# Low parts by accumulating DMAs, another place for M, and a table for side work, in a gated mix of linear attention and FNet

## The chip, the cores and the metric

The kernel runs on one core of one Trainium2 chip. The time is the device time of one execution in microseconds (us), the median of the runs shown. PE is TensorE, DVE is VectorE, ACT is ScalarE, POOL is GpSimd, SP is SyncE, which here only issues DMAs. A row such as `L748 PE MATMUL bank<-pk,c` is an instruction of line 748 of the kernel before; names are those of its tiles.

## The reference

S = 2048 tokens, D = 576, 32 heads of 18. All in float32.

```python
g = sigmoid((x * gate_w).sum(-1))
qkv = (x @ wqkv) split into q, k, v of 32 heads
phi = lambda t: where(t > 0, t + 1, exp(t)) + 1e-6
pq, pk = phi(q), phi(k)
kv = einsum("bhsd,bhse->bhde", pk, v); z = pk summed over s
o = einsum(pq, kv) / (einsum(pq, z) + 1e-6)
a = o @ wo
y = dft_seq_re @ (x @ dft_hid_re.T) - dft_seq_im @ (x @ dft_hid_im.T)
return g * a + (1 - g) * y
```

## The kernel before, in words

A float32 number is kept as two fp32r parts: `hi` (ACT copies the number into a tile of that type) and `lo` (DVE subtracts `hi` from the number). A product of two such numbers is three passes on PE: hi hi, hi lo, lo hi. Large products are built from seven smaller ones on sums of quarters: `Left` makes the seven left operands from pieces `xb` of x, `right_here` and `Hidden.make_w` the right operands `wb` and `wf`. The stages, in the order of time:

- **k'** (to about 65 us): x (tiles `xs`) times the key weights `wd`, sixteen tiles of 128 tokens, with phi on ACT and DVE, into `acc` (k' as numbers, for z) and `pk` (its parts).
- **k'^T x** (65 to 132 us): `pk` against x in the other layout, `c`, in 20 steps: five columns c by four quarters q. x comes by SP as `craw` and is split into `c`. Beside the steps runs side work: the sum of k' over its tiles (`zacc`, then `z_chain` and `z_sum`), the right operands of q (the three generators `wq_pieces`, a, b, c), the left operand `here[NP]` (p: its last rows go by SP from `xb` to a DRAM scratch, `xr<-xb`, and are read back as `rests[p]`, `xr<-xr`), the left operand of p = 6 (x), and the loads of Wo. `turn` says which generator is pushed at which step, `plan` what else is done there. `kv_step` multiplies by the value weights.
- **q** (129 to 195 us): 56 slots, eight pieces p by seven products (`q_product`, L913), each on two `xb` or `xf` parts and on `rests[p]`. Between slots stand, by a second `plan`, the making of kv, of M = kv Wo (`build_m` into `mf`), the moves of M's rows from `mf` into a layout of 128 rows by DMA (`move_m`; SP and POOL), M's parts (`split_m`), the left operands 7, 0 and 1 (`begin_left`, `left`), the loads of `rests` (`load_rest_q`), and the steps of the division by the denominators (`norm`, `pz`, `den`).
- **M** (195 to 263 us): sixteen tiles, transposed `acc` (`qs`, split into parts) times M (`mw`), evicted by ACT with the gate and stored to `att` by POOL. Beside them `Hidden.make_w` splits the seven right operands `wf` of the hidden transform, one at a tile; those of 3 to 6 lie over `acc` tiles that have been stored.
- **Hidden and sequence transforms** (263 us to the end).

The order of rows on each engine is that of the code after a scheduler that keeps dependencies; POOL and SP each issue their DMAs in order. `lo_later` puts a subtraction on a list that `tick` empties. The generators yield between pieces, `go` pushes one by a step. Of places: a tile is bound to an address (`at`), so two tiles at one address wait for each other. In q, M's raw rows lie at T_AT + 25856 and 35072, over the sums `sets` of the first slots; `mf` lies at T_AT, where `begin_left(1)` puts the pieces of left operand 1; `rests[6]` and `rests[2]` of the step table lie over the temporaries of piece c.

Of the kernel before, what the change touches and what calls it, by code (L numbers as in the profile page):

```python
# [8 lines left out]
F = mybir.dt.float32  # L9
R = mybir.dt.float32r  # L10
# [126 lines left out]
def kernel(  # L137
# [112 lines left out]
    acc = [at(ACC_AT + i * D * 4, [P, D], F, "acc") for i in range(NT)]  # L250
# [305 lines left out]
    pace()  # L556
# [52 lines left out]
    zacc = at(CONST_AT + 3584, [P, D], F, "zacc")  # L609
    for i in range(FT, NT):  # L610
# [12 lines left out]
        if i in (10, 12, 14):  # L623
            add(zacc, zacc if i > 10 else acc[0], acc[i // 2 - 4])
# [86 lines left out]
    def load_forms(p, o, queue=nc.sync):  # L711
        t = forms[p] = at(o, [P, 7, 2, 2 * P], R, "xf")
        for a, b in ((2, 4), (0, 2), (4, 6), (6, 7)):
            queue.dma_start(out=t.bitcast(F)[:, a:b], in_=xforms[p][:, a:b])
# [8 lines left out]
    turns = dict(p=rest_forms(), a=wq_pieces[0], b=wq_pieces[1], c=wq_pieces[2], x=left_of(6, False))  # L723
    turn = {4: "p", 5: "p", 6: "p", 7: "p", 8: "pap", 9: "pa", 10: "pax", 11: "pxa", 12: "paxc",
            13: "pcbx", 14: "xbc", 15: "bc", 16: "b", 17: "b"}

    plan = {
        2: [lambda: begin_left(NP, ACC_AT)],
        6: [z_chain, lambda: begin_left(6, ACC_AT + 22784)],
        8: [z_sum, lambda: go(wq_pieces[1]), lambda: go(wq_pieces[2])],  # L730
        12: [lambda: load_wo(2)],
        14: [lambda: load_forms(2, ACC_AT + 8448, nc.gpsimd), lambda: load_wo(3)],
        16: [lambda: wo_split[2](lo_later), lambda: load_rest_q(6, SLOT_AT + 40320)],
        17: [lambda: wo_split[3](lo_later), lambda: load_rest_q(2, SLOT_AT + 43904)],
# [4 lines left out]
    for c in range(5):  # L739
        ps = [bank(), bank()]  # L740
        passes = FULL if c < KC else FULL[:2]
        for q in range(NCU):
# [17 lines left out]
            for i in (2 * step + 4, 2 * step + 5):  # L760
                if i < NT:
                    add(zacc, zacc, acc[i])
            for f in plan.get(step, ()):
                f()
            left_part()
            for k in turn.get(step, ""):
                go(turns[k])
# [6 lines left out]
    for f in turns.values():  # L774
        go(f, 9)
# [30 lines left out]
    def scale(t, d):  # L806
# [3 lines left out]
        o = (SLOT_AT + (14336 if t < 3 else 48256) if t < 4 else T_AT + 36864) + t % 8 * 512  # L810
# [55 lines left out]
    def move_m(g, queue=nc.sync):  # L866

        if not ms:
            ms["raw"] = at(T_AT + 25856, [P, KC, D], F, "mraw")
            ms["rest"] = at(T_AT + 35072, [P, D], F, "mraw")  # L870
        mraw, mrest = ms["raw"], ms["rest"]
# [621 lines left out]
```

## Time and profile before

| | before |
|---|---|
| runs, us | 730.86 to 732.08, median 731.05 |
| the profiled execution, us | 731.42 |
| its span, us | 729.6 |
| around the span, us | 1.8 |
| PE busy | 719.6 us, 99% |
| DVE, ACT, POOL busy | 597.3, 329.6, 56.8 us |
| DMA | 211 GB/s over the span |
| mean PE clock | 0.997 of full |

A row of the timeline has start, duration, engine, line, operation and tiles; in brackets stands how long the engine was idle before it, and what it waited for. In a DMA row the last figure is the median time from issue to landing. The numbers of the windows are busy us (x instructions) of PE, PE's weight load, DVE, ACT and POOL, then PE's granted clock, the share of the DMA engines and GB/s.

### The profile page before, as it was taken

The page shows a single profiled execution, that of the slowest core. Times are in us where ns is not written, and L with a number is a line of the kernel's source. Part 1 is how long each engine was busy: PE and PEld are TensorE (multiplying, and loading weights), DVE is VectorE, ACT ScalarE, POOL GpSimd, SP SyncE. Part 2 cuts the span into 40 slices and gives each one's busy share as a digit, 9 for nine tenths or more (in the row PEclk, how much of TensorE's full clock was granted, in tenths as well). Part 3 has the DMA queues.
Part 4 walks back from the last instruction along what each step waited for, and adds up shares of the span by engine and source line. Part 5 has one row for each costly group of instructions (what it writes and reads, how often), then busy time and mean ns, then how long its engine had stood idle before and what let it go on. Part 6 is the DMA issues. An engine that isn't in the chain of part 4 may idle for free.

```text
span 729.6 us, 13716 instructions
## 1 busy us (share of the span) xinstructions
PE 719.6 (99%) x5390; PEld 715.8 (98%) x5390; DVE 597.3 (82%) x996; ACT 329.6 (45%) x506; POOL 56.8 (8%) x101
## 2 busy tenths in 40 slices
PE   9999999998999999999999999999999999999997
PEld 9999999998999999999999999999999999999997
DVE  5799987577999848979999889857888987788884
ACT  6898346575545544443344334323535332232230
POOL 1111221122041100000000000000000000000000
PEclk9999999999999999999999999999999999999999
DMA  7384798984279648454476666889964544544540
GB/s 255 115 279 163 246 302 296 396 276 175 102 260 384 263 147 329 130 161 137 155 247 175 223 240 199 290 308 400 374 198 132 159 140 141 159 150 144 153 152 33
DMA packets 51516, 156.66 MB, mean 215 GB/s; under 512 B 6212, under 2 KB 8676, under 8 KB 50428
## 3 DMA queue, kind: packets, MB, share of 16 engines
q1 hardware_dynamic: 42268, 116.43, 47.3%
q0 software_dynamic: 8896, 38.95, 14.7%
q8 instruction: 43, 0.70, 0.4%
q10 hardware_dynamic: 288, 0.41, 0.2%
q14 instruction: 21, 0.17, 0.1%
HBM read 117.80 MB, written 36.49 MB: 211 GB/s over the span
## 4 chain that ended last, share of the span: by engine, by line
PE 76%; DVE 10%; DMA 9%; issue 2%; ACT 1%; SPq 1%; POOL 1%; DVEq 0%; POOLq 0%; ACTq 0%
PE bank L1270 41%; PE bank L1115 14%; PE bank L209 14%; DMA xr<-xr 2%; DVE c L189 2%; PE bank L913 2%; PE bank L748 2%; PE bank L571 2%; DVE craw L199 1%; DVE fl L189 1%; DMA wraw<-in_wq_rest_dram 1%; DMA craw<-in_xg_dram 1%; DMA xm<-xb 1%; DVE ys L199 1%; PE bank L828 1%
## 5 line engine op out<-in xcount | busy, mean ns | idle before, releaser
L1270 PE MATMUL bank<-fh,c 128*128 128x288 f32 x1792 | 356.1, 295 | 0.4 <-DVE c L189 0.4
L1270 PEld LDWEIGHTS bank<-fh,c 128*128 128x128 f32 x1792 | 286.0, 188 | 1.0 <-DVE c L189 0.9
L1270 PE MATMUL bank<-fl,c 128*128 128x288 f32 x896 | 263.2, 294 | 0.4 <-DVE fl L189 0.4
L179 ACT ACTIVATE c<-craw 128x1792 fp32r<-128x1792 f32 (+1 forms) x84 | 121.6, 1448 | 192.8 <-DVE craw L199 158.4
L1270 PEld LDWEIGHTS bank<-fl,c 128*128 128x128 f32 x896 | 168.7, 188 | 1.1 <-DVE fl L189 0.9
L189 DVE TENSOR_TENSOR c<-craw,c 128x1792 fp32r<-128x1792 f32 (+4 forms) x86 | 141.9, 1653 | 1.7 <-ACT c L179 1.6
L199 DVE TENSOR_TENSOR craw<-craw 128x256 f32<-128x256 f32 (+1 forms) x192 | 98.3, 512 | 24.3 <-DMA craw<-in_ci_dram 13.0
L1115 PE MATMUL bank<-wf,xf 128*128 128x288 f32 x630 | 98.5, 296 | 0.0
L1115 PEld LDWEIGHTS bank<-wf,xf 128*128 128x128 f32 x630 | 90.0, 189 | 0.0
L209 PE MATMUL bank<-mw,qs 128*128 128x288 f32 x448 | 63.5, 298 | 0.8 <-DVE qs L189 0.5
L748 PE MATMUL bank<-pk,c 128*128 128x288 f32 x448 | 62.1, 296 | 0.8 <-ACT c L179 0.4
L748 PEld LDWEIGHTS bank<-pk,c 128*128 128x128 f32 x448 | 60.1, 188 | 1.5 <-DVE c L189 0.8
L209 PEld LDWEIGHTS bank<-mw,qs 128*128 128x128 f32 x448 | 60.0, 188 | 1.4 <-DVE qs L189 0.7
L209 PE MATMUL bank<-wd,xs 128*128 128x288 f32 (+1 forms) x336 | 44.7, 295 | 0.0
L209 PEld LDWEIGHTS bank<-wd,xs 128*128 128x128 f32 x336 | 44.6, 188 | 0.0
L199 DVE TENSOR_TENSOR ys<-bank,ys 128x288 f32<-128x288 f32 x63 | 28.8, 456 | 17.3 <-PE bank L1270 14.3
L189 DVE TENSOR_TENSOR fl<-fl,fh 128x864 fp32r<-128x864 f32 (+1 forms) x32 | 34.6, 1092 | 6.8 <-ACT fh L179 5.2
L179 ACT ACTIVATE fh<-fl 128x864 fp32r<-128x864 f32 (+1 forms) x32 | 29.8, 949 | 16.2 <-DVE fl L199 16.2
L1115 PE MATMUL bank<-wf,xr 96*128 96x288 f32 x112 | 33.3, 298 | 0.0
L199 DVE TENSOR_TENSOR ys<-ys,bank 128x288 f32<-128x288 f32 x47 | 21.1, 450 | 13.5 <-PE bank L1270 12.9
L1292 ACT ACTIVATE ys<-bank 128x288 f32<-128x288 f32 x16 | 6.6, 412 | 53.2 <-PE bank L1270 53.2
L1333 ACT ACTIVATE acc<-bank,gate 128x288 f32<-128x288 f32 x32 | 15.9, 502 | 29.7 <-PE bank L209 29.6
(131 smaller groups left out, 802.1 us busy)
## 6 DMA issues: line engine op xcount, KB each, us to landing
xf<-xm SPq DMA_DIRECT2D x49, 512.0 KB, 9.0
craw<-in_cr_dram SPq DMA_DIRECT2D x32, 512.0 KB, 3.8
craw<-in_ci_dram SPq DMA_DIRECT2D x32, 512.0 KB, 4.2
xr<-xr SPq DMA_DIRECT2D x20, 448.0 KB, 8.2
xm<-xb POOLq DMA_DIRECT2D x8, 1024.0 KB, 5.2
xm<-xb POOLq DMA_DIRECT2D x8, 768.0 KB, 7.1
craw<-in_xg_dram SPq DMA_DIRECT2D x20, 256.0 KB, 5.9
att<-acc POOLq DMA_DIRECT2D x16, 288.0 KB, 3.5
```

What stands on the lines that cost most here:

```text
L179: return nc.scalar.activation(dst, src, AF.Copy, bias=bias)
L189: nc.vector.tensor_tensor(out=dst, in0=src, in1=hi, op=ALU.subtract)
L199: nc.vector.tensor_tensor(out=dst, in0=a, in1=b, op=op)
L209: nc.tensor.matmul(ps, a, b, start=(n == 0), stop=(n == len(pairs) - 1))
L571: nc.tensor.matmul(ps[i], x[:, i * P:(i + 1) * P], wkt.row(h, j), start=(c == 0 and n == 0), stop=(c == KC and n == 1))
L748: nc.tensor.matmul(ps[h][:, :HALF], t[:, a, k], pk[s][:, b, half(h)], start=(s == 0 and n == 0), stop=(s == NT - 1 and n == len(passes) - 1))
L828: nc.tensor.transpose(banks[c // KC][:, (c % KC) * P:(c % KC + 1) * P], a, ident)
L913: nc.tensor.matmul(ps, a, b, start=(start and n == 0), stop=(stop and n == len(ops) - 1), skip_group_check=True)
L1115: nc.tensor.matmul(ps, a, b, start=(start and n == 0), stop=(n == len(ops) - 1), skip_group_check=True)
L1270: nc.tensor.matmul(ps[q], c[x][:, l, k], factors[p](y, f), start=(p == 0 and i == 0), stop=(p == NP - 1 and i == 2))
L1292: nc.scalar.activation(c11, ps[1], AF.Copy)
L1333: done.append(nc.scalar.activation(acc[i][:, half(h)], ps[:, :HALF], AF.Copy, scale=gate[:, t:t + 1]))
```

## The change

- **`lo_by_dma`**: the low part is made without DVE. ACT writes -hi into its place, and POOL issues a DMA that adds the raw number there. In `Hidden.make_w` it replaces DVE's fourteen subtractions of Wr's parts, one of 128 x 576 and one of 32 x 288 for each of seven; the sixth `make_w` goes from tile 12 to 13.
- **M**: raw rows go to T_AT + 14336 and 23552 (Wo's pieces 0, 1 and 4 lay there), all at slot 14 (before: 18 and 19). Its parts are made by chunk pairs: hi at slots 21 and 24, the rest at 28, the low parts by -hi on ACT and an accumulating DMA of 576 KB at 30 and 32 (before: DVE, at 31 and 46).
- **Slots in q**: `begin_left(1)` at 16 (19), `rests` 7 and 1 by SP (POOL), `rests` 5 by POOL ahead of its `xf` forms (SP; the forms were at slot 13, now 15), nine norms instead of ten and earlier ones, two `pz` places instead of four.
- **Sum of k'**: by pairs of tiles (128 x 1152): seven adds and a last one of 128 x 576, instead of fifteen of 128 x 576. `z_chain` stands at step 4 (6), `z_sum` at 7 (8).
- **Side work of k'^T x**: one table `turn` names what is done at each step. The stores of p's rest rows come a step later, piece a ends at step 15 (12). `rests[2]` goes to POOL, ahead of the forms of 2, both at step 16.

**Where the rows stand.** PE, the end of k'^T x and the first q products; `wb` are right operands of q, `xr_203` (after) and `xr_212` (before) are `rests[6]`, `c` the last two chunks of x. Before:

```order
L689 MATMUL bank_987<-gt_211_1636,plain_189_1396 72x72
L748 MATMUL bank_1639<-pk_42_123,c_205_1590 128x288 x2
L748 MATMUL bank_1640<-pk_42_123,c_205_1590 128x288 x2
...
L913 MATMUL bank_1771<-wb_104_481,xb_177_1260 128x288 x3
L748 MATMUL bank_1639<-pk_46_127,c_210_1631 128x288 x2
...
L748 MATMUL bank_1640<-pk_49_130,c_210_1631 128x288 x2
L913 MATMUL bank_1771<-wb_184_1346,xb_177_1260 128x288 x3
L913 MATMUL bank_1771<-wb_186_1350,xr_212_1663 128x288
L913 MATMUL bank_1784<-wb_104_481,xf_206_1592 128x288 x3
```

After:

```order
L703 MATMUL bank_979<-gt_202_1616,plain_177_1370 72x72
L929 MATMUL bank_1758<-wb_180_1374,xb_163_1166 128x288 x2
L929 MATMUL bank_1758<-wb_182_1378,xr_203_1644 128x288
L764 MATMUL bank_1619<-pk_34_115,c_197_1567 128x288 x2
L764 MATMUL bank_1620<-pk_34_115,c_197_1567 128x288 x2
...
L764 MATMUL bank_1619<-pk_41_122,c_201_1607 128x288 x2
L764 MATMUL bank_1620<-pk_41_122,c_201_1607 128x288 x2
L929 MATMUL bank_1771<-wb_96_473,xf_205_1648 128x288 x3
```

The first matmul on `rests[6]` stood behind the last 32 matmuls on `c`; now it stands ahead of them.

SP, the last steps of k'^T x: `xr<-xb` are the stores of the rest rows, `xr<-xr` the loads of `rests` (first the one of 6), `in_xg_dram` x for the steps. Before:

```order
L402 DMA xr_114<-xb_1095 32x4x896
L596 DMA craw_1588<-in_xg_dram 128x512
L662 DMA wraw_1598<-in_wo_dram 128x576
L596 DMA craw_1629<-in_xg_dram 128x512
L709 DMA xr_1663<-xr_114 128x896
L709 DMA xr_1696<-xr_114 128x896
L709 DMA xr_1717<-xr_114 128x896
```

After:

```order
L408 DMA xr_106<-xb_1084 32x4x896 x2
L602 DMA craw_1565<-in_xg_dram 128x512
L408 DMA xr_106<-xb_1084 32x4x896
L676 DMA wraw_1578<-in_wo_dram 128x576
L602 DMA craw_1605<-in_xg_dram 128x512
L723 DMA xr_1644<-xr_106 128x896
L723 DMA xr_1702<-xr_106 128x896
```

The last store stood ahead of the x load that is now ahead of it; the load of `rests[2]` is gone from here to POOL.

SP, in q, where `mf` is the source of M's moves, the last load of forms before them, and the first `xr<-xr` behind is `rests[0]`. Before:

```order
L721 DMA xf_1761<-xm_109 128x1536
L721 DMA xf_1762<-xm_110 128x1536
L709 DMA xr_2045<-xr_114 128x896
L709 DMA xr_2047<-xr_114 128x896
...
L880 DMA mraw_2081<-mf_1741 112x576
L880 DMA mraw_2081<-mf_1741 8x576 x2
L882 DMA mraw_2082<-mf_1741 64x576
```

After:

```order
L735 DMA xf_1749<-xm_102 128x1536
L892 DMA mw_2016<-mf_1726 4x576
L892 DMA mw_2016<-mf_1726 112x576
...
L894 DMA mraw_2017<-mf_1726 64x576
L895 DMA mraw_2017<-mf_1726 64x576
L723 DMA xr_2043<-xr_106 128x896
L723 DMA xr_2244<-xr_106 96x896
L723 DMA xr_2246<-xr_106 128x896
```

Nine moves that stood behind the loads of `rests` 0 and 5 now stand ahead of those of `rests` 0, 7 and 1.

The diff, cut to its core:

```diff
+    def lo_by_dma(dst, src, hi):
+        nc.scalar.activation(dst, hi, AF.Copy, scale=-1.0)
+        nc.gpsimd.dma_start(out=dst.bitcast(F), in_=src, accum_op=ALU.add)
...
-    acc = [at(ACC_AT + i * D * 4, [P, D], F, "acc") for i in range(NT)]
+    pairs = [at(ACC_AT + i * D * 4, [P, 2 * D], F, "acc") for i in range(0, NT, 2)]
+    acc = [pairs[i // 2][:, i % 2 * D:i % 2 * D + D] for i in range(NT)]
...
     zacc = at(CONST_AT + 3584, [P, D], F, "zacc")
+    sums = pairs[4]
+    z_at = {10: 0, 11: 1, 13: 2}
...
             f()
-        if i in (10, 12, 14):
-            add(zacc, zacc if i > 10 else acc[0], acc[i // 2 - 4])
+        if i in z_at:
+            add(sums, sums, pairs[z_at[i]])
...
+    z_left = [3, 5, 6, 7]
+    def z_pair():
+        add(sums, sums, pairs[z_left.pop(0)])
     def z_chain():
+        add(zacc, sums[:, :D], sums[:, D:])
...
-    turns = dict(p=rest_forms(), a=wq_pieces[0], b=wq_pieces[1], c=wq_pieces[2], x=left_of(6, False))
-    turn = {4: "p", 5: "p", 6: "p", 7: "p", 8: "pap", 9: "pa", 10: "pax", 11: "pxa", 12: "paxc",
-            13: "pcbx", 14: "xbc", 15: "bc", 16: "b", 17: "b"}
+    turns = {"p": rest_forms(), "a": wq_pieces[0], "b": wq_pieces[1], "c": wq_pieces[2],
+             "x": left_of(6, False), "L": left_part, "+": z_pair, "S": z_chain, "Z": z_sum,
+             "N": lambda: begin_left(NP, ACC_AT), "X": lambda: begin_left(6, ACC_AT + 22784),
+             "q": lambda: (go(wq_pieces[1]), go(wq_pieces[2]))}
+    turn = ("+L", "L+", "+N", "L", "+LSX", "LpL", "pL", "ZLpL", "pp", "qL", "pax", "axp", "pc", "ppca",
+            "xpacbx", "axbcb", "b", "", "b", "")
...
     plan = {
-        2: [lambda: begin_left(NP, ACC_AT)],
-        6: [z_chain, lambda: begin_left(6, ACC_AT + 22784)],
-        8: [z_sum, lambda: go(wq_pieces[1]), lambda: go(wq_pieces[2])],
         12: [lambda: load_wo(2)],
-        14: [lambda: load_forms(2, ACC_AT + 8448, nc.gpsimd), lambda: load_wo(3)],
-        16: [lambda: wo_split[2](lo_later), lambda: load_rest_q(6, SLOT_AT + 40320)],
-        17: [lambda: wo_split[3](lo_later), lambda: load_rest_q(2, SLOT_AT + 43904)],
+        14: [lambda: load_wo(3)],
+        16: [lambda: wo_split[2](lo_later), lambda: load_rest_q(6, SLOT_AT + 40320),
+             lambda: load_rest_q(2, SLOT_AT + 43904, nc.gpsimd),
+             lambda: load_forms(2, ACC_AT + 8448)],
+        17: [lambda: wo_split[3](lo_later)],
...
                 wvt[c + 1], wv_split = load_pair(wv_ring.next(), wv[:, c + 1])
-            for i in (2 * step + 4, 2 * step + 5):
-                if i < NT:
-                    add(zacc, zacc, acc[i])
+            for k in turn[step]:
+                turns[k]() if k in "+SNXZqL" else go(turns[k])
...
                 f()
-            left_part()
-            for k in turn.get(step, ""):
-                go(turns[k])
...
     tick()
-    for f in turns.values():
-        go(f, 9)
+    for k in "pabcx":
+        go(turns[k], 9)
...
                                        op0=ALU.add, op1=ALU.mult)
-        o = (SLOT_AT + (14336 if t < 3 else 48256) if t < 4 else T_AT + 36864) + t % 8 * 512
+        o = (SLOT_AT + (14336 if t < 3 else 48256) if t < 4 else T_AT + 38912) + t % 4 * 512
...
         if not ms:
-            ms["raw"] = at(T_AT + 25856, [P, KC, D], F, "mraw")
-            ms["rest"] = at(T_AT + 35072, [P, D], F, "mraw")
-        mraw, mrest = ms["raw"], ms["rest"]
+            ms["lo"] = at(T_AT + 14336, [P, KC, D], R, "mw")
+            ms["rest"] = at(T_AT + 23552, [P, D], F, "mraw")
+        mraw, mrest = ms["lo"].bitcast(F), ms["rest"]
...
+    minus = [at(T_AT + o, [P, 2, D], F, "minus") for o in (45568, 60416)]
     def split_m(h, part):
-        if h == 0 and part == 0:
-            ms["hi"] = at(T_AT + 14336, [P, 5, D], R, "mw")
-            ms["lo"] = at(T_AT + 25856, [P, KC, D], R, "mw")
-        mraw, mrest, mhi, mlo = (ms[k] for k in ("raw", "rest", "hi", "lo"))
+        if not part and not h:
+            ms["hi"] = at(T_AT + 25856, [P, 5, D], R, "mw")
+        mraw, mrest, mhi = ms["lo"].bitcast(F), ms["rest"], ms["hi"]
+        cs = slice(2 * h, 2 * h + 2)
         if part == 0:
-            hi_of(mhi[:, :KC, half(h)], mraw[:, :, half(h)])
-            hi_of(mhi[:, KC, half(h)], mrest[:, half(h)])
+            hi_of(mhi[:, cs], mraw[:, cs])
+        elif part == 1:
+            nc.scalar.activation(minus[h], mhi[:, cs], AF.Copy, scale=-1.0)
+            nc.gpsimd.dma_start(out=mraw[:, cs], in_=minus[h], accum_op=ALU.add)
         else:
-            lo_of(mlo[:, :, half(h)], mraw[:, :, half(h)], mhi[:, :KC, half(h)])
-            lo_of(mhi[64:, KC, half(h)], mrest[64:, half(h)], mhi[64:, KC, half(h)])
+            hi_of(mhi[:, KC], mrest)
+            lo_by_dma(mhi[64:, KC], mrest[64:], mhi[64:, KC])
...
     def spread():
-        pz_ring.at = [T_AT + 40960 + k * D * 4 for k in range(4)]
-    m_parts = [lambda: split_m(0, 0), lambda: split_m(0, 1),
-               lambda: split_m(1, 0), lambda: split_m(1, 1)]
+        pz_ring.at = [T_AT + 40960 + k * D * 4 for k in range(2)]
+    m_parts = [lambda a=a: split_m(*a) for a in ((0, 0), (1, 0), (0, 1), (1, 1), (0, 2))]
...
         12: [lambda: build_m((4,))],
-        13: [lambda: load_forms(5, T_AT + 66048, nc.gpsimd)],
-        15: [lambda: load_rest_q(0, SLOT_AT + 40320), lambda: load_rest_q(5, SLOT_AT + 43904)],
-        18: [lambda: move_m(2), lambda: move_m(0, nc.gpsimd), lambda: move_m(3)],
-        19: [lambda: move_m(4), lambda: move_m(1, nc.gpsimd), lambda: begin_left(1, T_AT)],
+        14: [lambda: move_m(2), lambda: move_m(0, nc.gpsimd), lambda: move_m(3), lambda: move_m(4),
+             lambda: move_m(1, nc.gpsimd)],
+        15: [lambda: load_rest_q(0, SLOT_AT + 40320),
+             lambda: load_rest_q(5, SLOT_AT + 43904, nc.gpsimd),
+             lambda: load_forms(5, T_AT + 66048)],
+        16: [lambda: begin_left(1, T_AT)],
...
         30: [spread],
-        31: [lambda: load_rest_q(7, T_AT + 80384, nc.gpsimd),
-             lambda: load_rest_q(1, T_AT + 108928, nc.gpsimd)],
+        31: [lambda: load_rest_q(7, T_AT + 80384), lambda: load_rest_q(1, T_AT + 108928)],
...
     }
-    for k, what in ((7, (10, 11, 13, 15, 17)), (0, (14, 16, 18, 20, 24)), (1, (33, 34, 35, 36, 38)),
-                    (None, (25, 27, 29, 41, 43, 45, 47, 48, 49, 52)), ("m", (30, 31, 45, 46))):
+    for k, what in ((7, (10, 11, 12, 15, 17)), (0, (13, 15, 17, 19, 23)), (1, (30, 33, 34, 36, 38)),
+                    (None, (18, 20, 25, 35, 41, 43, 47, 48, 48)), ("m", (21, 24, 30, 32, 28))):
...
                 f()
-            if k == 51:
+            if k == 52:
...
             hi_of(rl[:96], last)
-            lo_later(w[:, :, 1], raw, w[:, :, 0])
-            lo_later(rl[32:64], last[32:64], rl[32:64])
+            lo_by_dma(w[:, :, 1], raw, w[:, :, 0])
+            lo_by_dma(rl[32:64], last[32:64], rl[32:64])
...
         tick()
-        if i == 0 or 2 < i < 7:
+        if i in (0, 3, 4, 5, 6):
...
                 here[k].store((slice(0, 4), slice(4, 7))[j % 2], done[-1])
-        for k, j in enumerate((7, 8, 9, 10, 11, 12, 14)):
+        for k, j in enumerate((7, 8, 9, 10, 11, 13, 14)):
...
```

More of the change, by code (lines that the diff above doesn't have):

```diff
@@ L555 @@
         load_next()
-    pace()
+    pace(mybir.EngineType.Pool)
     for h in range(2):
@@ L709, in load_rest_q, with load_forms @@
         queue.dma_start(out=rests[p].bitcast(F)[:n], in_=xrest[p * 96:p * 96 + n])
-    def load_forms(p, o, queue=nc.sync):
-        t = forms[p] = at(o, [P, 7, 2, 2 * P], R, "xf")
+    def load_forms(p, o):
+        forms[p] = at(o, [P, 7, 2, 2 * P], R, "xf")
         for a, b in ((2, 4), (0, 2), (4, 6), (6, 7)):
-            queue.dma_start(out=t.bitcast(F)[:, a:b], in_=xforms[p][:, a:b])
+            nc.gpsimd.dma_start(out=forms[p].bitcast(F)[:, a:b], in_=xforms[p][:, a:b])
     def load_two(*places):
```

## The prediction

> **What bounds the kernel now.** I read the page first, then PE's waits by line, then the timeline and the chain at the waits. PE is the bound:
>
> ```profile
> PE 719.6 (99%) x5390; PEld 715.8 (98%) x5390; DVE 597.3 (82%) x996; ACT 329.6 (45%) x506; POOL 56.8 (8%) x101
> ```
>
> No matmul is removed, so only PE's stalls can be won or added. Its waits between 60 and 265 us (us in total, times, longest):
>
> ```profile
> PE bank L913 <- DVE xb L189: 1.1, 1, 1.1
> PE bank L913 <- DMA xr<-xr: 1.1, 2, 0.8
> PE bank L209 <- DVE qs L189: 0.5, 1, 0.5
> PE bank L748 <- ACT c L179: 0.4, 1, 0.4
> PE bank L209 <- ACT qs L179: 0.4, 1, 0.4
> PE bank L748 <- DVE c L189: 0.4, 1, 0.4
> ```
>
> That is 3.9 us, and all that this stretch offers beside a clock loss. The PE timeline (start, duration, idle before) shows the places that matter:
>
> ```profile
> 126.75 2.37 PE L748 MATMUL bank<-pk,c 128*128 128x288 f32 x16
> 131.92 0.30 PE L913 MATMUL bank<-wb,xr 96*128 96x288 f32 x1
> 133.37 0.40 PE L913 MATMUL bank<-wb,xr 96*128 96x288 f32 x1 [0.35 <-DMA xr<-xr]
> 160.07 0.30 PE L913 MATMUL bank<-wb,xr 96*128 96x288 f32 x1
> 174.25 0.96 PE L913 MATMUL bank<-wb,xf 128*128 128x288 f32 x6
> 176.75 0.82 PE L913 MATMUL bank<-wb,xb 128*128 128x288 f32 x4 [1.15 <-DVE xb L189]
> 178.35 0.40 PE L913 MATMUL bank<-wb,xr 96*128 96x288 f32 x1 [0.79 <-DMA xr<-xr]
> 179.91 1.64 PE L913 MATMUL bank<-wb,xf 128*128 128x288 f32 x6
> ```
>
> The same six matmuls take 0.96 us at 174.25 and 1.64 at 179.91: after 1.94 us of waits PE also ran at a lower clock. The windows (PE busy and count first, PEclk third from the end) give its size: 5 x (1 - 0.90) + 5 x (1 - 0.75) = 1.75 us.
>
> ```profile
> 175.00:180.00 5.00, 3.07 (x18) 2.60 (x17) 3.81 (x7) 3.64 (x10) 0.00 (x0) 0.90 0.44 161
> 180.00:185.00 5.00, 5.00 (x31) 5.00 (x31) 4.78 (x11) 3.26 (x8) 0.73 (x2) 0.75 0.01 3
> ```
>
> The waits at 176.75 and 178.35 therefore cost 1.15 + 0.79 + 1.75 = 3.7 us. The chain tells whence they come:
>
> ```profile
> 156.10 0.38 DVE acc L923
> 156.50 0.73 SPq L880
> ...
> 162.19 3.85 DMA mraw<-mf
> 166.81 0.64 POOL xb L366
> ...
> 170.38 7.93 DMA xr<-xr
> 178.35 4.74 PE bank L913 x22
> ```
>
> M's raw rows go onto the place of q sums, which DVE frees at 156.10; the left operand 1 is loaded over their source, so it starts only when they landed.
>
> **The change part by part.** The rows of SP's queue and of landings (KB each, median us to landing) that the terms use:
>
> ```profile
> 114.71 0.52 SPq L402 DMA_DIRECT2D xr<-xb  x1
> 118.22 0.34 SPq L596 DMA_DIRECT2D craw<-in_xg_dram  x1
> 122.77 4.49 SPq L709 DMA_DIRECT2D xr<-xr  x3
> 151.02 1.25 SPq L709 DMA_DIRECT2D xr<-xr  x2
> 156.50 5.07 SPq L880 DMA_DIRECT2D mraw<-mf  x7
> 161.61 0.54 SPq L882 DMA_DIRECT2D mraw<-mf  x1
> 162.19 0.59 SPq L883 DMA_DIRECT2D mraw<-mf  x1
> ...
> xr<-xr SPq DMA_DIRECT2D x20, 448.0 KB, 8.2
> xr<-xb SPq DMA_DIRECT2D x6, 448.0 KB, 7.8
> xr<-xr POOLq DMA_DIRECT2D x1, 336.0 KB, 4.7
> att<-acc POOLq DMA_DIRECT2D x16, 288.0 KB, 3.5
> xf<-xm POOLq DMA_DIRECT2D x6, 512.0 KB, 6.4
> ```
>
> *1. M elsewhere, moved at slot 14: -3.7.* The moves no longer wait for 156.10; they follow slot 14, at about 146 us if the 56 slots fill 129 to 195 evenly, and their region (Wo's pieces, last read at slot 12) is free by then. The xb loads behind them come some 7 us earlier than 166.81, far more than the 1.94 us of waiting, and rests 1 goes out on SP at slot 31, by the same spacing at about 166 us, instead of 170.38. Cover, if it is gone: the old 3.7. Bounds -3.7 and -1.2 (only the wait on xb goes).
>
> *2. SP's nine moves ahead of rests 0: +1.8.* Rests 0 and 5 were issued at 151.02, with the moves behind them; now the nine moves, 5.07 + 0.54 + 0.59 = 6.2 us of SP, come first, and behind them wait the loads of rests 0, 7 and 1 (rests 5 went to POOL). The matmul that reads rests 0 stood at 160.07; 151.02 + 8.2 = 159.2, so 0.9 us were to spare. If the moves start at 147.5 us (an estimate between 146, the even spacing, and 150), rests 0 goes out at 153.7 and lands at 161.9: 1.8 us late. Bounds: 146 gives 0.3; 150 gives 4.3; nothing, if the landing takes the 4.7 us of the 336 KB row.
>
> *3. Rests 6 is read earlier, and its load is later: +3.5, and +1.5 of clock.* In the new order PE meets the first matmul on rests 6 ahead of the last 32 matmuls on c. Their first half stood at 126.75, so PE comes there at 126.75 + 2 x 0.13 = 127.0, not at 131.92. The load waits for the last store xr<-xb. That store stood at 114.71, ahead of the xg load of 118.22; now it stands behind it, at about 118.6. With 7.8 us to landing the load goes out at 126.4 instead of 122.77, and with 8.2 it lands at 134.6: 7.6 us of stall. Other end: the store lands in time, the load goes out at 122.8 and takes 4.7: 127.5, 0.5 us. The xf loads of form 2, ahead of it in POOL's queue before, now leave after it or with it, which speaks for the shorter landings; I take 130.5, a stall of 3.5. The two waits of 1.94 us together were followed by 1.75 us of clock loss, so I add 1.5 (0 to 1.8). The wait of 0.35 at 133.37 goes: rests 2 is on POOL and is read after the 32 matmuls, 4.3 us later: -0.35. Behind PE's wait are queued the 32 matmuls on c, whose operands are ready; they fill no gap, since PE runs in order.
>
> The Trainium skill ("TensorE: Matmul & The Clock Gate", Part 1: The HAM clock gate) puts the drop to half clock at an idle window of some 3.4 us; here it came after two waits of 1.15 and 0.79 us, so the trace is the stricter. By the page the 1.5 us of clock would be nothing for a wait of under 3.4 us, which is rival C below.
>
> *4. z by pairs, and the turn table: -0.2.*
>
> ```profile
> L199 DVE TENSOR_TENSOR zacc<-zacc,acc 128x576 f32<-128x576 f32 x14 | 10.5, 750 | 0.2
> L189 DVE TENSOR_TENSOR mw<-mraw,mw 128x1152 fp32r<-128x1152 f32 x2 | 2.7, 1354 | 0.5 <-ACT mw L179 0.5
> L189 DVE TENSOR_TENSOR wf<-wraw,wf 128x576 fp32r<-128x576 f32 x7 | 5.3, 752 | 3.4 <-ACT wf L179 3.4
> L179 ACT ACTIVATE wf<-wraw 128x576 fp32r<-128x576 f32 x7 | 4.7, 676 | 0.0
> ```
>
> Fifteen adds of 0.75 us become seven of 1.35 (the 128x1152 row) and one of 0.75: 11.2 against 10.2 us, 1 us of DVE less in a stage where PE waited 0.8 us for c. The side work moves some steps later, towards the steps where these waits were. I take a quarter of the 0.8; bounds -0.8 and +0.6 (one more such wait).
>
> *5. M's and the q stage's DVE work: -0.8.* Four DVE lows (2.7 us for two of 128x1152, 0.9 for two of 64x288) go to ACT and POOL, one division step of ten is dropped, and DVE is busy 4.78 of 5 us in 180 to 185. The waits of 0.5 and 0.4 on qs stand at the end of that stretch; I take 0.8 of the 0.9; bounds -0.9 and 0. The replacing ACT copies are three, the two larger twice the 676 ns row's width, and ACT works 3.26 of 5 us there; the accumulating DMAs leave POOL when DMA moves 3 GB/s.
>
> *6. Wr's lows by DMA: +0.3.* Fourteen DVE subtracts (5.3 us for seven, and seven small ones) go; fourteen ACT copies like the 0.68 us row and fourteen POOL issues come, into tiles 7 to 14. There DVE is not late for anything, so their leaving gives nothing:
>
> ```profile
> 230.00:240.00 10.00, 10.00 (x80) 10.00 (x79) 8.64 (x18) 6.73 (x18) 1.62 (x3) 1.00 1.02 416
> ```
>
> DMA, however, is full (share 1.02), and ACT also evicts PE's banks. Four of the new pieces lie over tiles whose store to att must land first; the store stands behind the accumulating DMAs on POOL, and behind the ACT copy that waits stand the evictions. Bounds: 0 where ACT's slack hides it, and 2 x 2.9 = 5.8 where two stores land after 6.4 instead of 3.5 us. I take 0.3, by the 3.3 of 10 us that ACT has free in that window.
>
> The Trainium skill ("Collectives: The Full Stack", Why ReduceScatter is half of AllGather) speaks against this part: an add inside the DMA needs two source reads and so halves the rate. No row of before has an accumulating DMA. By the page 288 KB would go like 576 KB, nearer to the 6.4 us than to the 3.5 us row, and the term would be nearer 3 than 0.3.
>
> The other moves (transposes one group later, first products of the next stage ahead of the last tile, norms at other slots, a pz ring of two) change the order within a PE that is full there: 0, within 0.3 either way.
>
> **Sum.** -3.7 + 1.8 + 3.5 + 1.5 - 0.35 - 0.2 - 0.8 + 0.3 = +2.05 us. The profiled execution took 731.42 us (span 729.6 and 1.8 around it), 0.37 above the median of 731.05; so 733.5 for such an execution, and 733.1 for the median.
>
> **The rivals.** *A: both rests are in time (faster).* If stores and loads land in 5 rather than 8 us, since fewer transfers share the queues, the stall at rests 6 is 0.5 to 1, rests 0 costs nothing and the clock stays: -3.7 + 0.7 - 0.35 - 0.2 - 0.8 + 0.3 = -4.05, 727.0. It decides at a landing of rests 6 before 128.5 us. For it: the 4.7 us row; against: 20 loads of this kind with a median of 8.2. Chance 0.27. *B: the accumulating DMAs take double* and hold ACT in tiles 9 to 14: +2.05 + 4, 737.1. It decides where a store lands over 6 us after its issue. Chance 0.11. *C: the stalls come, but the clock stays*, as it would where a single wait of 3.5 us is too short to lower it: +2.05 - 1.5 = +0.55, 731.6, no change; against it the 0.75 of the window after two shorter waits. Chance 0.14. *D: the change doesn't do what it says*: the moves are still held, by SP or by their region, and the waits at 176.75 and 178.35 stay: +5.7, 736.8. Against it: the new place is free after slot 12. Chance 0.06. My forecast keeps 0.42.
>
> **How the numbers follow.** Likeliest: 733.1 us. A difference of 0.2% (1.46 us) is about what a measurement of this kernel can tell from no change: faster is below 729.6, slower above 732.5. Of the forecast's 0.42, 0.33 lie above, 0.06 within, 0.03 below (term 3 alone runs from 0.5 to 7.6); of C's 0.14, 0.12 within and 0.02 below. Faster 0.27 + 0.03 + 0.02 = 0.32; same 0.06 + 0.12 = 0.18; slower 0.33 + 0.11 + 0.06 = 0.50. Signs are mixed, so the forecast's own range, with the bounds of terms 2 and 3, is 731.5 to 738. The range for all reaches from A's 727.0 less 0.5 to B with term 3 in its middle: 726.5 to 738.5.
>
> **What would show it.** Term 1: no wait near 176 to 178 and PEclk 1.00 in 180 to 185. Term 2: a PE wait on xr near 160 after an SP issue at 153 or later. Term 3: a PE wait on xr near 127 ahead of 32 matmuls on c, and a clock under 1 behind it. Term 5: no wait on qs near 199. Term 6: no PE wait on ACT in 230 to 260, and landings of wf<-wraw near 3.5 us. The prediction is wrong if rests 6 lands before PE comes to it, or if ACT is held in the tiles.

## The result and the profile after

| | before | after |
|---|---|---|
| median of five runs, us | 730.86 | 736.43 |
| runs, us | 729.91 to 732.08 | 735.28 to 738.15 |
| profiled execution, span, us | 731.42, 729.6 | 735.28, 733.6 |

The ratio is 1.0078, interval 1.0059 to 1.0098: slower, by 5.6 us in the medians and 3.9 us in the profiled executions. PE is as busy as before, DVE 11.6 us less, ACT 10.2 us and POOL 17.5 us more:

```profile
PE 719.1 (98%) x5390; PEld 715.8 (98%) x5390; DVE 585.7 (80%) x971; ACT 339.8 (46%) x522; POOL 74.3 (10%) x118
```

PE's waits of 0.3 us and more, over the whole of after (us in total, times, longest); the first two are new:

```profile
PE bank L929 <- DMA xr<-xr: 3.5, 1, 3.5
PE bank L214 <- ACT qs L179: 3.3, 1, 3.3
...
PE bank L1286 <- DVE fl L189: 0.9, 2, 0.5
PE bank L577 <- ACT wd L179: 0.6, 1, 0.6
PE bank L764 <- DVE c L189: 0.4, 1, 0.4
PE bank L929 <- ACT wb L179: 0.3, 1, 0.3
```

Both traces hold 5390 matmuls. Where does the time go? I take the start of PE's n-th matmul and subtract that of the n-th matmul of before. The difference (us; the second column is when before is there) says in which stretch a kernel loses or gains; the other kernels are the experiments below.

| n | before at | after | wr_dve | wr_half | xr0_first | both | wr_alone | table_alone |
|---|---|---|---|---|---|---|---|---|
| 900 | 124 | -1.41 | -1.63 | -1.86 | -1.15 | -1.36 | -1.51 | -1.60 |
| 950 | 130 | -0.05 | -0.29 | -0.58 | 0.31 | -0.12 | -1.51 | 0.01 |
| 1150 | 157 | -0.38 | -0.66 | -1.07 | 0.45 | -0.25 | -2.13 | -0.48 |
| 1200 | 164 | 3.42 | 6.30 | 5.45 | 0.97 | 1.02 | -2.13 | -0.48 |
| 1350 | 188 | -0.59 | 2.30 | 1.45 | -0.09 | -1.21 | -3.79 | 1.41 |
| 1450 | 202 | -2.16 | 0.74 | -0.11 | -1.46 | -2.59 | -2.58 | 1.50 |
| 1800 | 247 | -2.12 | 0.79 | -0.06 | -1.45 | -2.36 | -2.57 | 1.50 |
| 1900 | 260 | 3.25 | 0.79 | -0.06 | 3.40 | -2.25 | 2.26 | 1.50 |
| 5380 | 724 | 3.95 | -0.18 | 0.04 | 2.44 | -2.36 | 3.06 | 2.18 |

At 247 us after is 2.1 us ahead of this execution of before. It loses 3.8 us at 157 to 164 and 5.4 at 247 to 260. The 0.7 us behind 260 lies in the later transforms, which the change doesn't touch; there the kernels differ by up to 1.0 us either way.

One trace of before is not all that before does. The kernel wr_alone changes nothing ahead of 228 us: each engine has the rows of before, in the same order. Yet it is 1.5 us ahead of before at 124 us and 2.6 at 202, further than after is. So a difference of 1 to 2 us in one stretch of this table need not come from an edit; the two losses are larger, and each has its wait.

**The loss near 160.** SP's queue and PE's timeline of after:

```profile
147.08 5.24 SPq L892 DMA_DIRECT2D mw<-mf  x7
152.44 0.54 SPq L894 DMA_DIRECT2D mraw<-mf  x1
153.02 0.59 SPq L895 DMA_DIRECT2D mraw<-mf  x1
154.12 0.49 SPq L723 DMA_DIRECT2D xr<-xr  x1
...
163.38 0.41 PE L929 MATMUL bank<-wb,xr 96*128 96x288 f32 x1 [3.53 <-DMA xr<-xr]
```

The chain of after has the landing in between, 9.22 us of it:

```profile
154.12 9.22 DMA xr<-xr
163.33 0.04 issue
163.38 6.68 PE bank L929 x48
```

**The loss near 250.** POOL's timeline of after (the bracket is its idle time before):

```profile
229.86 2.13 POOL L194 DMA_DIRECT2D wf<-wraw  x2 [1.03 <-ACT wf L193]
232.56 0.59 POOL L1351 DMA_DIRECT2D att<-acc  x1 [0.57 <-ACT acc L1349]
240.20 2.11 POOL L194 DMA_DIRECT2D wf<-wraw  x2 [7.06 <-ACT acc L1349]
241.48 1.43 POOL L1351 DMA_DIRECT2D att<-acc  x1
248.89 2.09 POOL L194 DMA_DIRECT2D wf<-wraw  x2 [5.99 <-issue]
```

The additions of tile 7 go out at 229.86, those of tile 8 at 240.20, 10.3 us later, though the tiles are 4.3 us apart. ACT had written -hi for them by 234.10, so the eviction that the bracket of 7.06 names, which ended at 239.68, is not what they needed. The store behind them goes out at 241.48; the eviction that it stores ended at 236.41 (235.91 + 0.50 below). From there the chain, ACT's timeline, and PE's:

```profile
241.48 8.24 DMA att<-acc
...
235.91 0.50 ACT L1349 ACTIVATE acc<-bank,gate 128x288 f32<-128x288 f32 x1 [0.48 <-PE bank L214]
...
249.80 1.02 ACT L179 ACTIVATE wf<-wraw 128x576 fp32r<-128x576 f32 x2 [4.88 <-DMA att<-acc]
251.88 0.77 ACT L179 ACTIVATE qs<-bank 128x512 fp32r<-128x512 f32 x2
...
252.53 3.77 PE L214 MATMUL bank<-mw,qs 128*128 128x288 f32 x17 [3.34 <-ACT qs L179]
```

ACT wants to write a piece of Wr over a stored tile, waits 4.88 us for that store, and the `qs` that PE needs stands behind on ACT. Then PE's clock falls, for 5 x (1 - 0.88) + 5 x (1 - 0.78) = 1.7 us:

```profile
250.00:255.00 5.00, 2.48 (x13) 2.31 (x14) 2.46 (x6) 4.14 (x10) 3.48 (x6) 0.88 0.63 132
255.00:260.00 5.00, 5.00 (x33) 5.00 (x32) 0.12 (x1) 2.22 (x5) 3.23 (x6) 0.78 0.75 147
```

**What was gained.** The waits near 176 and the lower clock behind them are gone:

```profile
175.00:180.00 5.00, 5.00 (x40) 5.00 (x39) 4.24 (x9) 3.94 (x11) 0.00 (x0) 1.00 1.06 224
180.00:185.00 5.00, 5.00 (x40) 5.00 (x39) 5.00 (x13) 2.46 (x7) 0.69 (x2) 1.00 0.52 103
```

### The profile page after: what moved, and what is told of

It reads as the page before. It is cut to its first block, busy times and chain, and to the rows that moved or that the text cites. A ratio compares the mean times of both kernels' runs of the same rounds, so it can differ in the third digit from the quotient of the medians.

```text
span 733.6 us, 13750 instructions
## 1 busy us (share of the span) xinstructions
PE 719.1 (98%) x5390; PEld 715.8 (98%) x5390; DVE 585.7 (80%) x971; ACT 339.8 (46%) x522; POOL 74.3 (10%) x118
## 3 DMA queue, kind: packets, MB, share of 16 engines
q0 software_dynamic: 11520, 42.71, 17.8%
## 4 chain that ended last, share of the span: by engine, by line
PE 81%; DMA 8%; DVE 7%; issue 2%; ACT 1%; SPq 0%; POOL 0%; DVEq 0%; ACTq 0%; POOLq 0%
PE bank L1286 41%; PE bank L1131 14%; PE bank L214 11%; PE bank L764 7%; PE bank L929 6%; DVE c L189 2%; DMA att<-acc 2%; PE bank L577 2%; DVE craw L204 1%; DMA xr<-xr 1%; DVE fl L189 1%; DVE ys L204 1%; DMA craw<-in_cr_dram 1%; DMA craw<-in_ci_dram 1%; DMA wraw<-in_wk_dram 1%
## 5 line engine op out<-in xcount | busy, mean ns | idle before, releaser
L214 PE MATMUL bank<-mw,qs 128*128 128x288 f32 x448 | 65.0, 302 | 3.3 <-ACT qs L179 3.3
L214 PEld LDWEIGHTS bank<-mw,qs 128*128 128x128 f32 x448 | 61.5, 192 | 3.7 <-ACT qs L179 3.6
L204 DVE TENSOR_TENSOR ys<-bank,ys 128x288 f32<-128x288 f32 x63 | 28.8, 457 | 18.5 <-PE bank L1286 15.3
L204 DVE TENSOR_TENSOR fl<-bank,y 128x288 f32<-128x288 f32 x48 | 21.7, 451 | 11.2 <-ACT y L1158 6.6
```

Source lines behind the costliest of these rows:

```text
L204: nc.vector.tensor_tensor(out=dst, in0=a, in1=b, op=op)
L214: nc.tensor.matmul(ps, a, b, start=(n == 0), stop=(n == len(pairs) - 1))
```

## The experiments

The theory: one loss is the order of SP's queue, the other the additions by DMA, which hold POOL's queue and through a store ACT. Each diff is against after unless another kernel is named. Each ratio is to executions of before taken along with the kernel; their medians run from 730.16 to 731.49 us, so kernels of different experiments compare by the ratios.

**wr_dve**: Wr's lows on DVE.

```diff
-            lo_by_dma(w[:, :, 1], raw, w[:, :, 0])
-            lo_by_dma(rl[32:64], last[32:64], rl[32:64])
+            lo_later(w[:, :, 1], raw, w[:, :, 0])
+            lo_later(rl[32:64], last[32:64], rl[32:64])
```

> After, with Wr's fourteen low parts subtracted on DVE as before. Theory (the accumulating DMAs hold POOL's queue, a store to att goes out late, ACT waits for its landing, PE for ACT): the wait of 3.3 us on qs near 252 and the lower clock behind it (15 matmuls, 1.6 us) go, the wait of 3.5 us on rests 0 near 160 stays: about 5.2 us under after, 731. Rival (the tiles are late because M's parts or the norms moved, not for Wr): the wait near 250 stays, within 1 us of after.

Measured 731.26 us, ratio to before 1.0018 (1.0004 to 1.0032). The loss of 5.4 at 247 to 260 is 0.0 in the table. The wait on `rests[0]` stays (4.3 us in this profile), and here the clock falls behind it. Together with a wait that is 0.8 us longer that costs 3.2 us more than in the profile of after (6.30 + 0.66 = 6.96 against 3.80):

```profile
160.00:165.00 5.00, 1.11 (x4) 1.11 (x5) 2.58 (x6) 1.40 (x5) 1.46 (x2) 0.75 0.76 271
165.00:170.00 5.00, 5.00 (x25) 5.00 (x25) 1.58 (x3) 3.02 (x7) 0.00 (x0) 0.57 0.17 56
```

**wr_plain**: the same DMAs without the addition, so that Wr's low parts are not computed.

```diff
-            lo_by_dma(w[:, :, 1], raw, w[:, :, 0])
-            lo_by_dma(rl[32:64], last[32:64], rl[32:64])
+            for dst, src, hi in ((w[:, :, 1], raw, w[:, :, 0]), (rl[32:64], last[32:64], rl[32:64])):
+                nc.scalar.activation(dst, hi, AF.Copy, scale=-1.0)
+                nc.gpsimd.dma_start(out=dst.bitcast(F), in_=src)
```

> After, with Wr's DMAs of the same bytes from the same queue but without the addition: the raw number lands over -hi, so Wr's low parts are not computed. Theory (the addition makes the transfer slow and fills the queue): landings of wf<-wraw near 2.5 us where they took 3.8, POOL not idle from 233 to 240, no wait on qs near 252: about 5 us under after. Rival (the place in POOL's queue and the saturated DMA engines do it, whatever the transfer is): landings of 8 to 10 us near 230 to 250 and the wait of 3.3 us stay, within 1 us of after.

Measured 731.96 us, 1.0018 (1.0002 to 1.0035): the wait near 252 is gone, so it is the addition, not the place in the queue or the bytes. The DMA engines are as full (a share of 1.03 in 230 to 240 us, 1.06 in after) and the landings no shorter (a median of 6.3 us, 3.9 in after), against the expectation. DVE, which would be another suspect, is as busy there (7.7 us, 7.4 in after). But in POOL's timeline of wr_plain the pair of the next tile follows after 4.3 us:

```profile
232.53 1.26 POOL L1102 DMA_DIRECT2D wf<-wraw  x2 [0.98 <-ACT wf L1101]
235.27 0.56 POOL L1352 DMA_DIRECT2D att<-acc  x1 [1.48 <-ACT acc L1350]
236.80 1.25 POOL L1102 DMA_DIRECT2D wf<-wraw  x2 [0.97 <-ACT wf L1101]
```

The fourteen issues keep POOL busy 8.7 us, with the addition 14.6. The means, 628 and 1251 ns, overstate the difference, since in after two issues in a row overlap (groups of wr_plain and of after):

```profile
L1102 POOL DMA_DIRECT2D wf<-wraw x14 | 8.7, 628 | 6.5 <-ACT wf L1101 4.7 <-PE bank L214 1.8
...
L194 POOL DMA_DIRECT2D wf<-wraw x14 | 14.6, 1251 | 19.9 <-ACT acc L1349 8.8 <-issue 6.0 <-ACT wf L193 2.6
```

**wr_alone**: before, with only this part (`lo_by_dma` in `make_w`, the sixth at tile 13).

> Before, with only Wr's lows by ACT and accumulating DMAs (and the sixth at tile 13). Theory (this part alone holds POOL's queue and through it ACT): a wait on ACT in the tiles near 245 to 250 with a lower clock behind, 4 to 5 us over before, as large as what taking it out of after gained (5.2). Rival (it hurts only together with the new M place or slots): under 1.5 us over before.

Measured 735.48 us, 1.0078 (1.0050 to 1.0105), 4.95 us over its before; in the table 4.8 us at 247 to 260. The two tests, taking the part out and putting it in alone, agree.

This trace also serves as a second one of before's rows up to 228 us. At the place where before waited 1.15 and 0.79 us and lost 1.75 us of clock, it waits as long and keeps the clock (PE's timeline and windows of wr_alone):

```profile
174.83 0.79 PE L918 MATMUL bank<-wb,xb 128*128 128x288 f32 x4 [1.35 <-DVE xb L189]
176.08 0.40 PE L918 MATMUL bank<-wb,xr 96*128 96x288 f32 x1 [0.46 <-DMA xr<-xr]
...
175.00:180.00 5.00, 4.54 (x33) 4.30 (x34) 4.87 (x12) 2.94 (x9) 0.00 (x0) 1.00 0.03 13
180.00:185.00 5.00, 5.00 (x40) 5.00 (x39) 4.99 (x10) 3.07 (x7) 1.06 (x2) 1.00 0.56 228
```

Of 98 executions of before timed with the experiments, 61 have a mean clock of 0.999 or more, where 1.75 us lost would leave 0.998; so the profile of before shows a loss that most of them don't have.

**wr_half**: half of each large addition, the rest on DVE.

```diff
-            lo_by_dma(w[:, :, 1], raw, w[:, :, 0])
-            lo_by_dma(rl[32:64], last[32:64], rl[32:64])
+            lo_by_dma(w[:, 0, 1], raw[:, 0], w[:, 0, 0])
+            lo_later(w[:, 1, 1], raw[:, 1], w[:, 1, 0])
+            lo_later(rl[32:64], last[32:64], rl[32:64])
```

> After, with only half of each of Wr's large lows by an accumulating DMA (128 rows of 288 columns), the rest on DVE: half the descriptors and one instead of two such DMAs a tile. Theory one (POOL holds a DMA back because too many descriptors of slow additions are in flight): the second addition goes out right after its ACT copy, no idle of 6 us on POOL, no wait on qs near 252: about 5 us under after, 731. Rival (an accumulating DMA isn't issued before the one before it has landed): POOL still idle until the landing of the first, a wait on ACT of 1 us or more in the tiles: within 3 us of after.

Measured 731.24 us, 0.9999 (0.9982 to 1.0016), with no wait in the tiles. POOL's timeline and DMA issues of wr_half:

```profile
231.61 0.88 POOL L194 DMA_DIRECT2D wf<-wraw  x1 [0.72 <-DVE den L809]
...
235.86 0.85 POOL L194 DMA_DIRECT2D wf<-wraw  x1 [0.70 <-ACT den L812]
...
wf<-wraw POOLq DMA_DIRECT2D x7, 144.0 KB, 6.8
```

The second addition goes out 4.25 us after the first, which lands only at 239.88, 8.3 us after its issue. So additions do not wait for each other by rule; half the bytes and one such DMA a tile are not held back. Nor are M's three in after, under way at once (issued at 169.26, 171.74 and 173.03, the first landing at 178.35), so the number of additions under way is not the limit by itself. Whether it is one of descriptors (Wr's two have 288 short rows a tile, each of M's at most 128 long ones) stays open.

**xr0_first**: `rests[0]` ahead of the moves.

```diff
-        14: [lambda: move_m(2), lambda: move_m(0, nc.gpsimd), lambda: move_m(3), lambda: move_m(4),
+        14: [lambda: load_rest_q(0, SLOT_AT + 40320), lambda: move_m(2), lambda: move_m(0, nc.gpsimd), lambda: move_m(3), lambda: move_m(4),
...
-        15: [lambda: load_rest_q(0, SLOT_AT + 40320),
-             lambda: load_rest_q(5, SLOT_AT + 43904, nc.gpsimd),
+        15: [lambda: load_rest_q(5, SLOT_AT + 43904, nc.gpsimd),
```

> After, with the load of rests 0 ahead of M's nine moves on SP. Theory (SP's queue): rests 0 goes out when its place is free, near 149.5, lands by 158, and the wait of 3.5 us near 160 goes: 3.5 to 4 us under after, about 732.5; the moves end near 156.5 and nothing waits for them. Rival (the engines are full with moves and forms, so that the landing takes 9 us or more from any place): it lands near 159 or later, 0 to 1 us of wait stay; second rival: the later moves bring back the waits near 176: the gain is under 1 us.

Measured 733.98 us, 1.0046 (1.0030 to 1.0062), about 1.5 us less gain than expected. The wait of 3.53 is gone (the 3.8 us lost at 157 to 164 became 0.5), and at matmul 1200 the kernel is 3.42 - 0.97 = 2.45 us ahead of after; at 1350 it is 0.5 behind. So the second rival was right in part: the moves end at 158.5 instead of 153.6, and PE waits 1.4 us for ACT's sums, 0.7 for forms and 0.5 for xb between 140 and 182. The gain in the times is larger than in the two profiles. The wait near 253 stays, as it should.

**both**: wr_dve and xr0_first together.

> Both edits together: Wr's lows on DVE and rests 0 ahead of the moves. Theory: the two stalls lie in different stages and add: 8.5 to 9 us under after, about 727.5, and 3 to 4 us under before, since M's move and the q stage's slots keep their gain of about 5 us and the k'^T x stage its 1.5. Rival (they share a resource): the sum falls short of the two by over 1.5 us.

Measured 729.01 us, 0.9986 (0.9968 to 1.0003). By the ratios the two edits add: 1.0078 - 1.0018 and 1.0078 - 1.0046 make 0.0092, and 1.0078 - 0.0092 is 0.9986. 727.5 was expected from the profiles; the gain over before in this one is 2.4 us. Timed again:

> The same kernel as both (Wr's lows on DVE, rests 0 ahead of the moves), timed in more rounds, since its interval of 0.9968 to 1.0003 left open whether it beats before. Its profile ended 2.3 us before that of before: theory, a ratio of 0.997 to 0.9985 with an interval under 1. Rival (the gain of that profile was a lucky one, the waits near 161 to 178 come with a lower clock in other executions): a ratio over 0.999.

Measured 729.05 us, 0.9976 (0.9964 to 0.9989): faster than before by 0.24%, and so than after; the interval of the first timing just reached 1. What is left of waits between 60 and 265 us:

```profile
PE bank L929 <- DMA xf<-xm: 0.9, 1, 0.9
PE bank L929 <- ACT sum L972: 0.8, 1, 0.8
PE bank L929 <- DVE xb L189: 0.5, 1, 0.5
PE bank L764 <- DVE c L189: 0.4, 1, 0.4
PE bank L929 <- ACT wb L179: 0.2, 1, 0.2
```

**table_alone**: before, with only the sum by pairs, the table, and the loads of step 16. It also has, as after has, POOL among the engines of `pace`, whose rows the code orders by hand.

> Before, with only the sum by pairs, the table of side work, and the loads of rests 2 and of the forms of 2 at step 16 on POOL. Theory (gains and losses of this stage cancel: the waits for c of 0.8 us and of 0.35 at 133 go, the early q products wait about 1.2 us on wb near 123): within 0.7 us of before, with the waits near 176 still there. Rival (the earlier read of rests 6 costs the 3.5 us that I forecast, and the profiled run of after only escaped it): a wait on xr near 127 and 2 us or more over before.

Measured 733.73 us, 1.0061 (1.0041 to 1.0080): neither theory. `rests[6]` costs nothing, and the stage ends 0.5 us ahead of before's trace, as expected (but 1.65 behind that of wr_alone). The loss comes later: the scheduler's new order reads `rests[1]` at matmul 1270 instead of 1291, 2.8 us of PE earlier, while its load is where it was. PE's timeline of table_alone:

```profile
177.04 0.61 PE L920 MATMUL bank<-wb,xr 96*128 96x288 f32 x1 [4.18 <-DMA xr<-xr]
177.45 1.64 PE L920 MATMUL bank<-wb,xb 128*128 128x288 f32 x6
```

**loads_first**: Wr on DVE, and all loads ahead of the moves (`rests` 5 by SP instead of POOL). The lines put in:

```diff
+        13: [lambda: load_forms(5, T_AT + 66048)],
+        14: [lambda: load_rest_q(0, SLOT_AT + 40320)],
+        15: [lambda: load_rest_q(5, SLOT_AT + 43904),
+             lambda: move_m(2), lambda: move_m(0, nc.gpsimd), lambda: move_m(3), lambda: move_m(4),
+             lambda: move_m(1, nc.gpsimd)],
```

> After with Wr's lows on DVE and, in q, the forms of 5 on POOL at slot 13 and rests 0 and 5 on SP ahead of M's moves (slots 14 and 15). Theory (order of the queues): the waits near 160 (rests 0; and on the forms of 5, 1.0 us, where rests 0 alone was put ahead) go, the moves end near 158, the left operand 1 is still 2 us early, no wait near 176: about 726.5, 0.5 to 0.6% under before. Rival (the moves land at 163 and later, and the waits near 176 come back): 728 to 730.

Measured 730.24 us, 1.0005 (0.9993 to 1.0018): the expectation missed by 3.7 us. The moves land at 163 to 164, and ACT, whose next instruction at slot 21 splits M, stands idle with the q sums behind it (its timeline); PE waits 2.6 us for sums and 1.5 for a rest:

```profile
163.69 1.17 ACT L179 ACTIVATE mw<-mw 128x1152 fp32r<-128x1152 f32 x1 [6.52 <-DMA mw<-mf]
```

**late_m** and **both_late**: loads_first and both, with M's steps later.

```diff
-("m", (21, 24, 30, 32, 28))
+("m", (27, 30, 36, 38, 34))
```

> The kernel with the loads first, and the steps that split M six slots later (27, 30, 34, 36, 38). Theory (ACT sits idle for 6.5 us at slot 21 until M's moves land, and the q sums behind it hold PE's banks): the waits of PE on ACT's sums between 165 and 174 (2.6 us of the 2.6 in that kernel) go: 2.5 to 3.5 us under loads_first, about 727. Rival (ACT has no room for M's seven pieces later either, or M is then late at 194): the waits move on, within 1 us of loads_first.

> Wr's lows on DVE, rests 0 ahead of the moves, and the steps that split M six slots later. Theory (in the kernel without the last edit ACT waited 2.1 us for M's moves, and PE 0.5 us for a sum; the forms of 5 come 1.0 us late in both): 0.5 to 1 us under that kernel, about 0.2 to 0.3% under before. Rival: the splitting of M now meets that of the left operand 1 on ACT (slots 30 to 38), and a wait on xb near 176 grows: 0.5 us over it or more.

Measured 731.50 us, 1.0003 (0.9991 to 1.0016), and 731.41 us, 1.0000 (0.9987 to 1.0013). The idle time moved, as the rival said: M's steps now meet those of left operand 1, and PE waits 3.6 and 3.1 us for a sum behind them (ACT's timeline of late_m, where the sum that PE needs starts at 178.12):

```profile
174.88 1.93 ACT L179 ACTIVATE xb<-xb 128x1024 fp32r<-128x1024 f32 x2 [4.15 <-DVE xb L204]
176.72 0.67 ACT L179 ACTIVATE mw<-mraw 128x576 fp32r<-128x576 f32 x1
177.41 0.68 ACT L193 ACTIVATE mw<-mw 64x576 fp32r<-64x576 f32 x1
178.12 0.41 ACT L972 ACTIVATE sum<-bank 128x288 f32<-128x288 f32 x1
```

**m_dve**: loads_first with M's lows by three DVE subtractions in place.

```diff
-            nc.scalar.activation(minus[h], mhi[:, cs], AF.Copy, scale=-1.0)
-            nc.gpsimd.dma_start(out=mraw[:, cs], in_=minus[h], accum_op=ALU.add)
+            lo_of(ms["lo"][:, cs], mraw[:, cs], mhi[:, cs])
...
-            lo_by_dma(mhi[64:, KC], mrest[64:], mhi[64:, KC])
+            lo_of(mhi[64:, KC], mrest[64:], mhi[64:, KC])
```

> The kernel with the loads first, and M's low parts subtracted on DVE in place (three subtractions instead of three ACT copies and three accumulating DMAs). Theory (M's accumulating DMAs are slow, 9 to 11 us each, but nothing waits for them, and they spare DVE 3.2 us in a stage where it is full): 0 to 1.5 us over loads_first, with waits on qs near 198 back. Rival (they cost as Wr's do, since the stores of the left operand behind them on POOL go late): 0.5 to 2 us under loads_first.

Measured 731.41 us, 1.0019 (1.0005 to 1.0032), 1.2 us over loads_first in the medians, with intervals that overlap: M's additions, slow as they are, do no harm, and may help a little. The waits on `qs` near 198, expected back with M's lows on DVE, did not come back.

## Why the prediction was right, and where its terms were off

Slower was right, and 736.43 lies in the range, which is 12 us wide; 733.1 was too low. Against the profiled 735.28 the sum gave 733.5. The mechanism was wrong by both of the signs that the prediction itself named: `rests[6]` landed (126.51) before PE came to it (127.54), and ACT was held in the tiles (4.88 us). By the table, term by term:

- *Term 1 (M elsewhere), -3.7*: measured 3.42 to -0.59 between 1200 and 1350, -4.0. The mechanism is right: the two waits are gone. The size is so against this trace of before alone, for 1.75 of it is the lower clock. In wr_alone that loss is missing, and the same stretch is 1.7 us shorter than in before without the edit; by either count the move itself takes away some 2.3.
- *Term 2 (rests 0 behind nine moves), +1.8*: +3.8, inside its bounds. The start at 147.08 and the nine moves were as forecast (154.12 against 153.7); the mis-sized steps are the landing, 9.22 us instead of 8.2, and the 0.4 us of issue.
- *Term 3 (rests 6), +3.5 and +1.5 of clock*: nothing. The order moved as said, and PE came at 127.54, but the last store landed 5.89 us after its issue (at 123.35), and the load took 3.03 us, not the median of 8.2, so it was there at 126.51. This is the step that failed: a median of twenty loads, most of them in fuller stretches, was taken for one. In before this load took 8.2 us too (122.77 to 130.93), but there POOL issued the loads of form 2 ahead of it, at 121.71, and in after behind it, at 124.56. The prediction had named that and still kept 3.5; that it is the cause was not tested. No kernel with the table waits there. The wait at 133 went, -0.45 (n = 950 to 1000) against -0.35, but wr_alone, without the table, doesn't have it either (-0.62). SP's and PE's timelines of after:

```profile
117.45 1.16 SPq L408 DMA_DIRECT2D xr<-xb  x1
...
123.48 4.23 SPq L723 DMA_DIRECT2D xr<-xr  x2
...
127.54 0.30 PE L929 MATMUL bank<-wb,xr 96*128 96x288 f32 x1
```

- *Term 4 (pairs and table), -0.2*: -1.4 until 124, both waits on c near 89 and 115 gone, then +1.4 near 123, where q products pulled ahead wait for `wb`, and `c` behind them is late (0.34 and 0.41 us idle). I had bounded the stage by -0.8 and +0.6 and named neither of the two sizes. Of the -1.4 only some 0.7, at the wait near 89, is the table's: the rest came in wr_alone too. Against that trace the stage loses 0.9 us (from 65 to 137), outside the bounds and of the other sign.
- *Term 5 (DVE relief), -0.8*: -1.6 between 1350 and 1450, beyond the bound of -0.9, and the two waits on `qs` are gone. The reason given fails in m_dve, which has M's lows on DVE and none of these waits. Which of the new slots in q removes them is not shown.
- *Term 6 (Wr's additions), +0.3*: +5.4, rival B, to which I gave 0.11. Its point of decision, a store that lands over 6 us after its issue, was met (8.24), but the larger part was that the store left 5 us late. I had priced the additions by their landing alone; the step that failed is the issue, since POOL held the next pair back until the pair ahead had landed. The lower clock behind the wait, 1.7 of the 5.4, was not in the term either.

So the sign came out right for half of the reasons, and the time by luck: a forecast stall that wasn't there (5.0) stood in the sum for one that I had held unlikely (5.1 short in term 6).

The median of after lies 1.15 us above its profiled execution, at a mean clock of 0.993 against 0.998. The lower clock behind the wait on `rests[0]`, seen in wr_dve and not in the profile of after, would do that; the other executions have no trace, so it isn't shown.

## What to carry to other kernels

Work taken from an engine that waits for nothing buys nothing: the 8 us or so of DVE work lifted from the tiles had no one waiting for them, and the DMAs that replaced them had. When a DMA is put on a queue, price three things: what the issue costs the engine, what stands behind it, and who waits for what stands behind it; here a store, then ACT, then PE. And when a table moves reads, look at the loads of all that is read later too: the order can pull a read ahead of its load two stages on, as with `rests[1]` in table_alone.

## What the runs showed of the hardware

- An addition in a DMA moved bytes at half the rate or less. In 177 to 184 us of after only M's additions are under way: a share of 0.80 of the engines for 159 GB/s, against 1.02 for 416 in the window that the prediction shows: (0.80 / 159) / (1.02 / 416) = 2.05 times the engine time per byte. Wr's own transfers agree: POOL's queue took 15.8% of 729.4 us of the 16 engines in wr_dve, 16.7% of 730.4 in wr_plain and 17.8% of 733.6 in after, so the same bytes cost 6.7 us plain and 15.3 with the addition, 2.3 times.

```profile
177.00:184.00 7.00, 7.00 (x55) 7.00 (x54) 7.00 (x15) 4.22 (x12) 0.00 (x0) 1.00 0.80 159
```

  The Trainium skill ("Collectives: The Full Stack", Why ReduceScatter is half of AllGather) has a ReduceScatter at half the rate of an AllGather because its add needs two source reads, and measured 1.93; the rate here agrees, the reads no run shows.
- It costs POOL more time to issue (2.1 us for a pair against 1.26). And with two such DMAs a tile POOL issued the next pair only when the first DMA of the pair ahead had landed (239.87 and 240.20, 248.57 and 248.89), though no wait in the trace says so. It did so each time: all six later pairs of after, of wr_alone and of xr0_first left 0.31 to 0.34 us after that landing, also behind 252 us, where a landing took 3.9 us and not 8 to 10.
- A wait of 3.5 to 4.3 us is followed by a lower clock in one execution and not in the other, at the same matmul: 0.57 in wr_dve at 165 to 170 us (above), 1.00 in after. In wr_plain and wr_half, with waits of 4.4 and 3.9 us, it was 0.57 and 0.67. Where a trace here shows the lower clock before the end of the span, it is half the clock for 3.4 us (before from 179.0 us: 0.51) or 6.8 us (wr_dve from 162.5: 0.50). The Trainium skill ("TensorE: Matmul & The Clock Gate", Part 1: The HAM clock gate) has the idle window of 3.4 us run freely; that would fit, and that waits of 1.15 and 0.79 us within 3 us lowered it in before does not; in wr_alone those of 1.35 and 0.46 us did not lower it.

```profile
165.00:170.00 5.00, 5.00 (x39) 5.00 (x39) 3.01 (x7) 4.86 (x11) 1.85 (x3) 1.00 0.39 133
```
